# Seven token tiles in place of eight, the last three 512 wide, in a fused attention and two-block feed-forward kernel

## The chip, the cores and the metric

The kernel runs on one core of a Trainium2 chip. The metric is the device time of one execution in microseconds. Three runs of the kernel before took 1172.88, 1173.68 and 1174.52 us (median 1173.68). TensorE is called PE, VectorE DVE, ScalarE ACT, GpSimd POOL and SyncE SP.

## The reference

All inputs are float32. Stage one is a chunked attention over 4 batches, 8 heads, 768 positions of 64 values: the queries of a chunk of 32 positions see 8 memory keys and the keys from 16 positions before the chunk to 8 behind it.

```
scores = q_c @ [mem_k, k_ctx]^T / 8;  a = softmax(scores);  o = a @ [mem_v, v_ctx]
x  = o as 3072 tokens x 512
h  = x @ w_in                          # 512 -> 2048
g  = max(h, 0) + log1p(exp(-|h|))      # softplus
x1 = g @ w_out                         # 2048 -> 512
out = ((x1 @ w_a) * (x1 @ w_b)) @ w_out2   # 512 -> 1536 -> 512
```

## The kernel before, in words

Every product is made of three matmuls on a high and a low part of each operand, which keeps float32 precision.

**Token tiles.** The 3072 tokens are cut into eight tiles of 384 (TT). For each tile t and each of 16 slices f of the hidden dimension one *iteration* runs: `emit_h` (12 matmuls into a PSUM bank `ph`, L563), `emit_soft` (ACT: Abs, Exp, Ln, L570 to L572; DVE: the final step into `g`, L574; ACT: the high part `gh`, L551; POOL, or DVE in the first and last tile: the low part `gl`, L554), and `emit_x1` of the iteration two before (12 matmuls into the four accumulator banks `px`, L587). Behind the last slice of a tile the four accumulators are copied by DVE (L595) and stored to a scratch (L596); that happens in the second iteration of the next tile, and the next tile's first `emit_x1` needs the copied banks.

**Attention beside it.** The attention of later tiles runs inside earlier tiles. It is cut into units of 128 tokens; units 0 to 5 come first, by other code, and units 6 to 23 go through the steps of the class `Unit`: `turn` (DVE transposes of keys and queries, L411 to L414, and two small ACT copies, L416), `scores` (PE, L430), `soft` (8 masked reductions on DVE, L379, and 8 exponentials on ACT, L383), `norm` (DVE, then POOL, L390), `flip` and `flip2` (5 DVE transposes each, L448), `values` (PE, L477, into a bank of the same pair as `ph`), `place` (ACT and DVE, writes the unit into the x tile of a later token tile).

**Order.** Time is counted in slots, two for an iteration: slot 2(16t+f) is reached behind `emit_soft`, the next one behind `emit_x1`. A list `plan` holds (slot, unit, step) and `att_at(slot)` emits what is due. From tile 1 on, SP, PE and DVE run in exactly the order in which the code emits; ACT and POOL are ordered by a planner. `placed[u]` is the slot of a unit's `values`, `scored[u]` that of its `scores` (the slot of `values` of the unit ahead), the others stand at fixed distances (L24, L25, L518). The same list holds `Early`: 30 conversions of later weights, each a fetch, an ACT step (`top`), a DVE step of two instructions (`value`, L685, L686) and a store. Keys and queries are fetched by many small DMAs per group of three units, values by two to four per unit.

**Stage two** takes x1 back in pairs of 512-token tiles and runs 12 slices of a 7-product scheme (L772) and the output product (L795), all with 512 columns.

Of the kernel before, what the change touches and what calls it, by code (L numbers as in the profile page):

```python
# [44 lines left out]
PRE, PRE_BY = 5, 4.2  # L45
PRE_STEPS = (0, 3.4, 4.1, 4.3)
# [4 lines left out]
def attn_moe_moe2(ctx: ExitStack, tc: tile.TileContext, q, k, v, mem_k, mem_v,  # L51
# [14 lines left out]
    UPT = TT // QU  # L66
    BPT = TT // QB
    KS = KB // 32
    NTILE = NT // TT
# [81 lines left out]
    masks = [ap.tile([P, KB], F32, name=f"mask{i}") for i in range(4)]  # L151
# [81 lines left out]
    def x_tile(t):  # L233
        if t not in xt:
            xt[t] = mp.tile([P, 2, KT, TT], F32R, tag="x", name=f"x{t}")
        return xt[t]
# [155 lines left out]
    class Unit:  # L392


        def __init__(self, u):
            self.u = u
            self.b, self.n = divmod(u, NU)
            self.own_bank = False

# [3 lines left out]

        def turn(self):
            u, kn, qn = self.u, loaded.k, loaded.q
# [4 lines left out]
            self.qt = a2.tile([P, KT, QU], F32, tag="qt", name=f"qt{u}", bufs=1)  # L410
# [69 lines left out]
        def place(self):  # L480
            t, c0 = divmod(self.u * QU, TT)
# [20 lines left out]
    placed = {u: 2 * NF1 * (u // UPT - 1) + PLACED[u % UPT] for u in range(2 * UPT, len(units))}  # L502
    scored = {u: placed[u - 1] if u > 2 * UPT else SCORED for u in placed}
    turned = {u: scored[u] + TURN if u > 2 * UPT else TURNED for u in placed}
# [22 lines left out]
    for t in range(2, NTILE):  # L527
# [13 lines left out]
    def turn_of(tag, n, dtype):  # L541

        if tag not in rings:
            rings[tag] = mp.tile([P, n, TT], dtype, tag=tag, name=tag, bufs=1)
# [4 lines left out]
    def split(val, name, engine=nc.gpsimd, between=None):  # L549
        hi, lo = turn_of("gh", 3, F32R), turn_of("gl", 3, F32R)  # L550
        anchor[0] = nc.scalar.copy(hi, val)  # L551
        if between:
            between()
        engine.tensor_tensor(lo, val, hi.bitcast(F32), ALU.subtract)  # L554
        return hi, lo

    def emit_h(t, f):
        x, w = xt[t], w1[f]
        ph = ps.tile([P, 512], F32, tag="h", name=f"ph{t}_{f}")[:, :TT]
# [8 lines left out]
    def emit_soft(t, f, ph, engine=nc.gpsimd, one=None, two=None):  # L568
        e = mp.tile([P, TT], F32, tag="e", name=f"e{t}_{f}")
# [7 lines left out]
        gt[t, f] = split(g, f"g{t}_{f}", engine, two)  # L577

    def emit_x1(t, f):
# [46 lines left out]
    def operand(p, n):  # L626
# [6 lines left out]
        if n in ("11", "s2", "s3"):  # L633
            return [home(f"x{n}", late["x"], [P, KH, 2, T2], f"x{n}")]
        if n == "s1":
            return [home("xs1a", late["x"], [P, 1, 2, T2], "xs1"), home("xa", mp, [P, 3, 2, T2], "x")[:, 0:1]]
        if n == "12":
            return [home("xa", mp, [P, 3, 2, T2], "x")[:, 1:3]]
        if n == "22":
            return [home("xb", mp, [P, 3, 2, T2], "x")[:, 0:2]]  # L640
        return [parts[p, "xb"][:, 2:3], home("xs4b", mp, [P, 1, 2, T2], "gh")]

    def pieces_of(p, n):
        k = 0
        for x in sums[p, n]:
            yield x, raws[n][:, k:k + x.shape[1]]
            k += x.shape[1]

    def split_hi(p, n, copy):
        sums[p, n] = operand(p, n)  # L650
        for x, raw in pieces_of(p, n):
            copy(x[:, :, 0], raw)

    def split_lo(p, n, engine):
        for x, raw in pieces_of(p, n):
            engine.tensor_tensor(x[:, :, 1], raw, x[:, :, 0].bitcast(F32), ALU.subtract)
# [122 lines left out]
    def temp(tag, name):  # L779
        return mp.tile([P, T2], F32, tag=tag, name=name, bufs=2 if tag == "e" else 1)  # L780
# [90 lines left out]
    def order():  # L871
# [62 lines left out]
        n_pre = PRE * (NTILE - 2)  # L934
        for n, e in enumerate(pre[:n_pre]):
            t, i = divmod(n, PRE)
            for d, step in zip(PRE_STEPS, (e.fetch, e.top, e.value, e.store)):
                plan.append((2 * NF1 * (t + 1) + PRE_BY * i + d, 100 + n, step))
# [25 lines left out]
        for t in range(NTILE):  # L964
# [9 lines left out]
            for f in range(NF1):  # L974
                ph = emit_h(t, f)
                if t == 0:
                    fetch_to(ROUNDS_CV + AHEAD + int(len(rest) * (f + 1) / CV_DONE))
                    convert()
                    emit_soft(t, f, ph, nc.vector, convert)
                    convert()  # L980
                elif t < NTILE - 1:
                    emit_soft(t, f, ph)
                else:
                    emit_soft(t, f, ph, nc.vector, partial(slot, 2 * f), partial(slot, 2 * f + 1))
                att_at(2 * (NF1 * t + f))
                if len(pend) >= LAG:
                    emit_x1(*pend.pop(0))
                pend.append((t, f))
                att_at(2 * (NF1 * t + f) + 1)
        def between_0():  # L990
            emit_x1(*pend.pop(0))

        for k in sorted(plan2):
            slot(k)
        for p in range(NPAIR):
            more = p + 1 < NPAIR
            for f in range(NF2):

                def at(k):
# [22 lines left out]
                    if more:  # L1022
# [4 lines left out]
                        if f == NF2 - 1:  # L1027
                            split_hi(p + 1, PRODUCTS[k], nc.scalar.copy)
                            if k > 0:
                                split_lo(p + 1, PRODUCTS[k - 1], nc.gpsimd if k in (2, 4) else nc.vector)  # L1030
                    if f == 0 and k == 0 and p > 0:
                        split_lo(p, PRODUCTS[6], nc.vector)
                    if p == f == 0 and k in (0, 2):
                        split_hi(0, PRODUCTS[5 + k // 2], nc.scalar.copy)
                    if p == f == 0 and k in (1, 3):
                        split_lo(0, PRODUCTS[5 + k // 2], nc.vector)
# [43 lines left out]
```

## Time and profile before

| what | before |
|---|---|
| median of three runs | 1173.68 us |
| the profiled execution | 1173.41 us |
| its span, first to last instruction | 1171.6 us |
| PE busy | 1161.1 us (99%) |
| DVE busy | 724.2 us (62%) |
| ACT busy | 530.7 us (45%) |
| POOL busy | 263.6 us (23%) |
| PE, share of the chain that ended last | 94% |

The profile is of one execution. Between the span and the time lie 1.8 us. A busy PE is a PE with matmuls in flight; the gap from one matmul's start to the next one's is the better measure. The stage of the token tiles lies from 40 to 633 us of the span, stage two behind it.

### The profile page before, as it was taken

The page shows a single profiled execution, that of the slowest core. Times are in us where ns is not written, and L with a number is a line of the kernel's source. Part 1 is how long each engine was busy: PE and PEld are TensorE (multiplying, and loading weights), DVE is VectorE, ACT ScalarE, POOL GpSimd, SP SyncE. Part 2 cuts the span into 40 slices and gives each one's busy share as a digit, 9 for nine tenths or more (in the row PEclk, how much of TensorE's full clock was granted, in tenths as well). Part 3 has the DMA queues.
Part 4 walks back from the last instruction along what each step waited for, and adds up shares of the span by engine and source line. Part 5 has one row for each costly group of instructions (what it writes and reads, how often), then busy time and mean ns, then how long its engine had stood idle before and what let it go on. Part 6 is the DMA issues. An engine that isn't in the chain of part 4 may idle for free.

```text
span 1171.6 us, 20283 instructions
## 1 busy us (share of the span) xinstructions
PE 1161.1 (99%) x7462; PEld 1049.1 (90%) x7462; DVE 724.2 (62%) x1603; ACT 530.7 (45%) x1293; POOL 263.6 (23%) x239
## 2 busy tenths in 40 slices
PE   9899999999999999999999999999999999999998
PEld 7799999999999999999999888888888888888887
DVE  6888655565555655455377567867456657455555
ACT  6899666656666566666565332222211113111110
POOL 2000223233232222322324665710002001000000
PEclk9999999999999999999999999999999999999999
DMA  9955353533534335332474758464854443864301
GB/s 228 301 189 103 90 135 76 132 80 98 132 79 125 81 104 136 75 101 68 140 261 161 274 216 287 171 224 150 339 203 144 152 145 106 305 226 153 135 1 72
DMA packets 193714, 181.47 MB, mean 155 GB/s; under 512 B 123168, under 2 KB 151760, under 8 KB 193616
## 3 DMA queue, kind: packets, MB, share of 16 engines
q1 hardware_dynamic: 193232, 180.13, 49.4%
q8 instruction: 59, 0.97, 0.3%
q14 instruction: 39, 0.32, 0.1%
q0 software_dynamic: 384, 0.05, 0.0%
HBM read 129.79 MB, written 50.33 MB: 154 GB/s over the span
## 4 chain that ended last, share of the span: by engine, by line
PE 94%; DMA 2%; DVE 1%; SPq 1%; ACT 0%; issue 0%; POOL 0%; DVEq 0%; POOLq 0%
PE px L587 22%; PE ph L563 22%; PE py L795 17%; PE pX L772 8%; PE pV L772 8%; PE pW L772 8%; PE pY L772 4%; PE pxa L477 2%; PE sc L430 1%; DMA raw<-in_moe_w_in_dram 1%; DMA vv<-in_v_dram 1%; DMA kp<-in_k_dram 1%; SPq L330 1%; DVE af L448 0%; PE pa L466 0%
## 5 line engine op out<-in xcount | busy, mean ns | idle before, releaser
L563 PE MATMUL ph<-x,w 128*128 128x384 f32 x1536 | 289.4, 336 | 0.1
L587 PE MATMUL px<-gh,w 128*128 128x384 f32 x1024 | 281.5, 335 | 1.4 <-DVE qn L295 1.4
L563 PEld LDWEIGHTS ph<-x,w 128*128 128x128 f32 x1536 | 267.2, 188 | 2.1 <-ACT x L369 0.2
L795 PE MATMUL py<-w2o,c 128*128 128x512 f32 (+1 forms) x870 | 218.0, 388 | 0.0
L795 PEld LDWEIGHTS py<-w2o,c 128*128 128x128 f32 x870 | 162.7, 188 | 33.5
L587 PEld LDWEIGHTS px<-gh,w 128*128 128x128 f32 x1024 | 186.7, 188 | 2.8 <-DVE qn L295 1.8
L574 DVE SCALAR_TENSOR_TENSOR g<-ph,e 128x384 f32<-128x384 f32 x128 | 71.0, 555 | 189.0 <-ACT e L572 184.9
L587 PE MATMUL px<-gl,w 128*128 128x384 f32 x512 | 171.1, 334 | 0.0
L854 ACT CAST c<-r 128x512 fp32r<-128x512 f32 x36 | 22.4, 622 | 308.2 <-DVE r L852 287.2
L554 POOL TENSOR_TENSOR gl<-g,gh 128x384 fp32r<-128x384 f32 x96 | 97.3, 1014 | 222.8 <-ACT gh L551 206.7
L551 ACT CAST gh<-g 128x384 fp32r<-128x384 f32 x128 | 65.6, 513 | 88.4 <-DVE g L574 87.2
L804 DVE TENSOR_TENSOR y<-py,y 128x512 f32<-128x512 f32 (+1 forms) x121 | 82.9, 685 | 36.2 <-PE py L795 36.0
L570 ACT ACTIVATE e<-ph 128x384 f32<-128x384 f32 x128 | 62.3, 486 | 88.4 <-PE ph L563 75.7
L587 PEld LDWEIGHTS px<-gl,w 128*128 128x128 f32 x512 | 96.1, 188 | 0.1
L448 DVE STREAM_TRANSPOSE af<-sm 32x256 f32<-32x256 f32 x180 | 78.2, 434 | 3.6 <-POOL sm L390 1.1
L572 ACT ACTIVATE e<-e 128x384 f32<-128x384 f32 x128 | 67.3, 526 | 3.9
L571 ACT ACTIVATE e<-e 128x384 f32<-128x384 f32 x128 | 67.3, 526 | 3.6
L851 DVE TENSOR_TENSOR d<-pW,q 128x512 f32<-128x512 f32 x36 | 24.9, 691 | 69.1 <-PE pW L772 69.1
L383 ACT ACTIVATE sm<-sm,st 128x96 f32<-128x96 f32 x168 | 60.5, 363 | 5.8 <-DVE st L379 5.8
L772 PE MATMUL pX<-x,u 128*128 128x512 f32 x216 | 54.8, 389 | 0.0
L772 PE MATMUL pW<-xs,u 128*128 128x512 f32 x216 | 54.8, 389 | 0.0
L772 PE MATMUL pY<-xs,u 128*128 128x512 f32 x216 | 54.8, 389 | 0.0
(162 smaller groups left out, 1634.8 us busy)
## 6 DMA issues: line engine op xcount, KB each, us to landing
u<-u_scratch SPq DMA_DIRECT2D x72, 512.0 KB
u_scratch<-u SPq DMA_DIRECT2D x36, 512.0 KB
w2o<-w2o_scratch SPq DMA_DIRECT2D x24, 512.0 KB
raw<-in_moe_w_in_dram SPq DMA_DIRECT2D x16, 512.0 KB
raw<-in_moe_w_out_dram SPq DMA_DIRECT2D x16, 512.0 KB
vn<-in_v_dram SPq DMA_DIRECT2D x35, 176.0 KB
raw_a<-in_moe_w_a_dram SPq DMA_DIRECT2D x12, 512.0 KB
raw_b<-in_moe_w_b_dram SPq DMA_DIRECT2D x12, 512.0 KB
```

The source lines that it names most:

```text
L448: nc.vector.transpose(out=af[32 * kb:32 * kb + 32, x], in_=self.sm[32 * x:32 * x + 32, :, 32 * kb:32 * kb + 32])
L551: anchor[0] = nc.scalar.copy(hi, val)
L554: engine.tensor_tensor(lo, val, hi.bitcast(F32), ALU.subtract)
L563: nc.tensor.matmul(ph, lhsT=w[:, a, kt * P:(kt + 1) * P], rhs=x[:, c, kt, :], start=n == 0, stop=n == 3 * KT - 1)
L570: nc.scalar.activation(e, ph, AF.Abs)
L571: nc.scalar.activation(e, e, AF.Exp, scale=-1.0)
L572: nc.scalar.activation(e, e, AF.Ln, bias=1.0)
L574: nc.vector.scalar_tensor_tensor(g, ph, 0.0, e, ALU.max, ALU.add)
L587: nc.tensor.matmul(acc[t][i][:, :TT], lhsT=a, rhs=c, start=f == 0 and m == 0, stop=f == NF1 - 1 and m == 2)
L772: nc.tensor.matmul(bank[:, :T2], lhsT=u[:, j, a, kt * P:kt * P + P], rhs=x[kt][:, c], start=first_ and m == 0, stop=m == 3 * KH - 1, skip_ ...
L795: nc.tensor.matmul(b, lhsT=c[:, x, r], rhs=w[:, y, cols], start=n == 0, stop=n == 3 * GROUP - 1)
L804: tt(y, b, y, ALU.add)
```

## The change

The token tiles become four of 384 and three of 512 (`WIDTHS`). The slots of `values` are written out by hand (`PLACED`): units 6 to 13 nine slots behind their `scores`, units 14 and 15 ten, units 16 to 23 eight, so that all units are placed by slot 190 of 224 (before: 222 of 256). The queries are turned by a step of their own (`turn_q`), five slots ahead of `scores`. The keys are turned three slots ahead of `scores` (two in 512-wide tiles) in place of two with the queries, and their buffer is now shared with the softmax's `sm`, so that they are turned behind the `flip2` of the unit in front. `flip` and `flip2` stand five and six slots behind `scores` (four and five where the unit has eight). DVE's result `g` is written over `e`; `gh` and `gl` have two buffers in place of three, and are emitted behind the `emit_x1` of the iteration. The copies of the accumulators go to a buffer of `tmp` and one of `e` in turn, behind `gh` and `gl`. The six conversions of a tile stand 5.1 slots apart (before: five, 4.2). In stage two the operands lie in two buffers of four parts, and some splits move by one position at the end of a pair.

```diff
+WIDTHS = (384, 384, 384, 384, 512, 512, 512)
-PLACED = (11, 21, 30)
+PLACED = (43, 52, 61, 70, 79, 88, 97, 106, 116, 126, 134, 142, 150, 158, 166, 174, 182, 190)
 TURNED, SCORED = 32, 34
-TURN, SOFT, NORM, FLIP, FLIP2 = -2, 1, 3, 5, 6
-HALVES = ((0, 8, 0.6), (8, 13, 0.9))
+TURN_Q, TURN, TURN_SOON, SOFT, NORM, FLIP, FLIP2 = -5, -2, -3, 1, 3, 5, 6
+HALVES = ((0, 8, 0.65), (8, 13, 0.9))
-PRE, PRE_BY = 5, 4.2
-PRE_STEPS = (0, 3.4, 4.1, 4.3)
+PRE, PRE_BY = (0, 6, 6, 6, 6, 6, 0), 5.1
+PRE_STEPS = (0, 4.4, 5.0, 5.2)
...
-            sm = a2.tile([P, H, KB], F32, tag="sm", name=f"sm{u}", bufs=1)
-            st = a2.tile([P, 4, H], F32, tag="st", name=f"st{u}")
+            sm = a2.tile([P, H, KB], F32, tag="kt", name=f"sm{u}", bufs=1)
+            st = a2.tile([P, 4, H], F32, tag="st", name=f"st{u}", bufs=1)
...
-    turned = {u: scored[u] + TURN if u > 2 * UPT else TURNED for u in placed}
+    turned = {u: TURNED if u == 2 * UPT else scored[u] + TURN if WIDTHS[units[u - 1].at] == T2 else scored[u] + TURN_SOON
+              for u in placed}
...
-        whens[i] = [(turned[u], "turn"), (at - 0.005, "scores"), (at + SOFT, "soft"), (at + NORM, "norm"),
-                    (max(at + FLIP, to - 7), "flip"), (max(at + FLIP2, to - 5), "flip2"), (to - 0.03, "values"), (to - 0.02, "place")]
+        whens[i] = [(max(at + TURN_Q, TURNED), "turn_q"), (turned[u], "turn"), (at - 0.005, "scores"), (at + SOFT, "soft"), (at + NORM, "norm"),
+                    (at + FLIP - (to - at < 9), "flip"), (at + FLIP2 - (to - at < 9), "flip2"), (to - 0.03, "values"), (to - 0.02, "place")]
...
     def emit_soft(t, f, ph, engine=nc.gpsimd, one=None, two=None):
-        e = mp.tile([P, TT], F32, tag="e", name=f"e{t}_{f}")
+        c = slice(0, WIDTHS[t])
+        e = turn_of("e", 2, F32)[:, c]
+        hi, lo = turn_of("gh", 2, F32R)[:, c], turn_of("gl", 2, F32R)[:, c]
...
-        g = turn_of("g", 2, F32)
-        nc.vector.scalar_tensor_tensor(g, ph, 0.0, e, ALU.max, ALU.add)
+        nc.vector.scalar_tensor_tensor(e, ph, 0.0, e, ALU.max, ALU.add)
...
+        def parts():
+            anchor[0] = nc.scalar.copy(hi, e)
+            if two:
+                two()
+            engine.tensor_tensor(lo, e, hi.bitcast(F32), ALU.subtract)
...
+                elif i % 2 == 0:
+                    o = mp.tile([P, n], F32, tag="tmp", name=f"xo{t}_{i}", bufs=2)
                 else:
-                    o = turn_of("g", 2, F32) if i > 1 else mp.tile([P, TT], F32, tag="e", name=f"xo{t}_{i}")
-                nc.vector.tensor_copy(o, acc[t][i][:, :TT])
-                nc.sync.dma_start(x1d[:, i, TT * t:TT * t + TT], o)
+                    o = turn_of("e", 2, F32)[:, :n]
+                nc.vector.tensor_copy(o, acc[t][i][:, :n])
+                nc.sync.dma_start(x1d[:, i, C0[t]:C0[t + 1]], o)
...
                 att_at(2 * (NF1 * t + f))
-                if len(pend) >= LAG:
-                    emit_x1(*pend.pop(0))
+                done = pend.pop(0) if len(pend) >= LAG else None
+                if done:
+                    emit_x1(*done)
+                parts_()
+                if done:
+                    emit_x1_out(*done)
                 pend.append((t, f))
```

## Rows read from the trace of the kernel before

**Rows 1.** The page: busy time by engine, and the granted clock in 40 slices.
```profile
PE 1161.1 (99%) x7462; PEld 1049.1 (90%) x7462; DVE 724.2 (62%) x1603; ACT 530.7 (45%) x1293; POOL 263.6 (23%) x239
...
PEclk9999999999999999999999999999999999999999
```

**Rows 2.** The page: the chain that ended last, by engine.
```profile
PE 94%; DMA 2%; DVE 1%; SPq 1%; ACT 0%; issue 0%; POOL 0%; DVEq 0%; POOLq 0%
```

**Rows 3.** The chain in order of time: start, us, what; each stage's commonest piece.
```profile
386.23 2.08 PE px L587 x12
...
800.90 1.36 PE py L795 x6
```

**Rows 4.** Waits of PE in the token tiles: total us, times, longest.
```profile
PE px L587 <- DVE qn L295: 1.4, 1, 1.4
...
PE sc L430 <- DVE qt L414: 1.0, 1, 1.0
```

**Rows 5.** Timeline of DVE, 376 to 404 us: start, us, instruction [idle before <- releaser].
```profile
380.40 2.22 DVE L448 STREAM_TRANSPOSE af<-sm 32x256 f32<-32x256 f32 x5
382.65 0.43 DVE L685 TENSOR_SCALAR val_a<-raw_a 128x512 uint32<-128x512 uint32 x1
...
383.91 2.23 DVE L448 STREAM_TRANSPOSE af<-sm 32x256 f32<-32x256 f32 x5
...
386.65 0.70 DVE L411 STREAM_TRANSPOSE kt<-kn 128x512 f32<-128x512 f32 x1
...
387.60 0.67 DVE L414 STREAM_TRANSPOSE qt<-qn 128x512 f32<-128x512 f32 x1
...
390.84 1.04 DVE L686 SCALAR_TENSOR_TENSOR val_b<-raw_b,val_b 128x512 uint32<-128x512 uint32 x1 [0.82 <-ACT raw_b L681]
...
394.75 0.25 DVE L379 CUSTOM_DVE_ANT_0 sm<-sc,mask 128x96 f32<-128x96 f32 x1
...
395.99 0.25 DVE L379 CUSTOM_DVE_ANT_0 sm<-sc,mask 128x96 f32<-128x96 f32 x1
```

**Rows 6.** Timeline of PE at the second tile's end: the group behind h, and two groups later.
```profile
200.52 0.33 PE L587 MATMUL px<-gh,w 128*128 128x384 f32 x1
...
204.68 0.33 PE L587 MATMUL px<-gh,w 128*128 128x384 f32 x1
```

**Rows 7.** Timeline of DVE there: softplus's last step, then the copies.
```profile
202.43 0.56 DVE L574 SCALAR_TENSOR_TENSOR g<-ph,e 128x384 f32<-128x384 f32 x1 [3.25 <-ACT e L572]
202.91 1.01 DVE L595 COPY xo<-px 128x384 f32<-128x384 f32 x2
203.84 0.55 DVE L595 COPY g<-px 128x384 f32<-128x384 f32 x1
```

**Rows 8.** Groups by form: busy us, mean ns of one | idle before.
```profile
L574 DVE SCALAR_TENSOR_TENSOR g<-ph,e 128x384 f32<-128x384 f32 x128 | 71.0, 555 | 189.0 <-ACT e L572 184.9 <-issue 3.4
...
L551 ACT CAST gh<-g 128x384 fp32r<-128x384 f32 x128 | 65.6, 513 | 88.4 <-DVE g L574 87.2
...
L383 ACT ACTIVATE sm<-sm,st 128x96 f32<-128x96 f32 x168 | 60.5, 363 | 5.8 <-DVE st L379 5.8
...
L843 DVE TENSOR_TENSOR r<-pV,r 128x512 f32<-128x512 f32 x36 | 24.9, 692 | 31.6 <-PE pV L772 31.6
...
L854 ACT CAST c<-r 128x512 fp32r<-128x512 f32 x36 | 22.4, 622 | 308.2 <-DVE r L852 287.2 <-issue 21.0
```

**Rows 9.** Timeline of ACT: the next iteration's Abs at that tile's end.
```profile
205.47 0.49 ACT L570 ACTIVATE e<-ph 128x384 f32<-128x384 f32 x1 [1.93 <-DMA x_scratch<-xo]
```

**Rows 10.** Timeline of SP: the copies' stores, and a fetch of queries.
```profile
203.48 0.83 SPq L596 DMA_DIRECT2D x_scratch<-xo  x2
...
401.91 0.43 SPq L191 DMA_DIRECT2D qn<-in_q_dram  x1
```

**Rows 11.** Timeline of ACT: the small key copies of unit 6.
```profile
124.86 0.34 ACT L416 COPY kt<-mem_t 128x32 f32<-128x32 f32 x2 [0.62 <-DVE kt L413]
```

**Rows 12.** Busy time by stretch, inside the first tile: PE, PEld, DVE, ACT, POOL.
```profile
75.00:98.00 23.00, 23.00 (x257) 22.59 (x248) 19.88 (x52) 21.18 (x53) 0.00 (x0) 1.00 0.70 225
```

More of the change, by code (lines that the diff above doesn't have):

```diff
@@ L66, in attn_moe_moe2 @@
     UPT = TT // QU
+    C0 = [sum(WIDTHS[:t]) for t in range(len(WIDTHS) + 1)]
     BPT = TT // QB
     KS = KB // 32
-    NTILE = NT // TT
+    NTILE = len(WIDTHS)
     NPAIR = NT // (2 * T2)
@@ L149, in next_half @@
         return halves[n_half[0] - 1]
-    masks = [ap.tile([P, KB], F32, name=f"mask{i}") for i in range(4)]
+    masks = [ap.tile([P, KB], F32, name=f"mask{i}") for i in range(3)]
+    masks.append(wp.tile([P, KB], F32, tag="w", name="mask3"))
     ident = wp.tile([P, P], F32, tag="w", name="ident")
@@ L480, in place @@
         def place(self):
-            t, c0 = divmod(self.u * QU, TT)
+            t = sum(self.u * QU >= c for c in C0[1:])
+            c0 = self.u * QU - C0[t]
             x = x_tile(t)
@@ L547, in turn_of @@
         return rings[tag][:, n_turn[tag] % n]
[L549 to L555, printed above, removed]
     def emit_h(t, f):
         x, w = xt[t], w1[f]
-        ph = ps.tile([P, 512], F32, tag="h", name=f"ph{t}_{f}")[:, :TT]
+        ph = ps.tile([P, 512], F32, tag="h", name=f"ph{t}_{f}")[:, :WIDTHS[t]]
         n = 0
@@ L624, in add_pair, with operand @@
             engine.tensor_tensor(r["s4"], r["12"], r["s2"], ALU.subtract)
-    def operand(p, n):
+    def operand(p, n, i):
         def home(key, pool, shape, tag):
@@ L633, in operand, with split_hi, split_lo @@
         if n in ("11", "s2", "s3"):
[L634 to L656, printed above, removed]
+            return home(f"x{n}", late["x"], [P, KH, 2, T2], f"x{n}")
+        x = home("xa" if n in ("s1", "12") else "xb", mp, [P, 4, 2, T2], "x")
+        return x[:, 0:2] if n in ("s1", "22") else x[:, 2:4]
+    PIECES = {n: 1 for n in PRODUCTS}
+    def split_hi(p, n, copy, which=(0, 1)):
+        for i in which:
+            if i < PIECES[n]:
+                x = operand(p, n, i)
+                sums.setdefault((p, n), []).append(x)
+                k = x.shape[1]
+                copy(x[:, :, 0], raws[n][:, i * k:i * k + k])
+    def split_lo(p, n, engine, which=(0, 1)):
+        for i in which:
+            if i < PIECES[n]:
+                x = sums[p, n][i]
+                k = x.shape[1]
+                engine.tensor_tensor(x[:, :, 1], raws[n][:, i * k:i * k + k], x[:, :, 0].bitcast(F32), ALU.subtract)
     us, w2o = {}, {}
@@ L779, in temp @@
     def temp(tag, name):
-        return mp.tile([P, T2], F32, tag=tag, name=name, bufs=2 if tag == "e" else 1)
+        if tag == "e":
+            return turn_of("e", 2, F32)
+        if tag == "g":
+            if "r" not in late:
+                late["r"] = late["x"].tile([P, T2], F32, name="r", bufs=1)
+            return late["r"]
+        return mp.tile([P, T2], F32, tag="gl", name=name, bufs=1)
     cs, yacc, jobs, n_jobs = {}, {}, [], [0]
@@ L933, in order @@
         pre = [Early(*divmod(n, 3)) for n in range(3 * NF2)]
-        n_pre = PRE * (NTILE - 2)
-        for n, e in enumerate(pre[:n_pre]):
-            t, i = divmod(n, PRE)
+        n_pre = sum(PRE)
+        for n, (t, i) in enumerate((t, i) for t in range(NTILE) for i in range(PRE[t])):
+            e = pre[n]
             for d, step in zip(PRE_STEPS, (e.fetch, e.top, e.value, e.store)):
-                plan.append((2 * NF1 * (t + 1) + PRE_BY * i + d, 100 + n, step))
+                plan.append((2 * NF1 * t + PRE_BY * i + d, 100 + n, step))
         plan.sort(key=lambda p: p[:2])
@@ L1027, in at @@
                         if f == NF2 - 1:
[L1028 to L1036, printed above, removed]
+                            for n, *which in HIGHS[k]:
+                                split_hi(p + 1, n, nc.scalar.copy, which or (0, 1))
+                            for n, engine in LOWS[k]:
+                                split_lo(p + 1, n, engine)
+                    if f == 0 and p > 0:
+                        for n in HIGHS_0[k]:
+                            split_hi(p, n, nc.scalar.copy)
+                        for n, engine in LOWS_0[k]:
+                            split_lo(p, n, engine)
+                    if p == f == 0:
+                        if k == 0:
+                            split_hi(0, "22", nc.scalar.copy)
+                        if k == 1:
+                            split_lo(0, "22", nc.vector)
+                        if k == 2:
+                            split_hi(0, "s4", nc.scalar.copy)
+                        if k == 3:
+                            split_lo(0, "s4", nc.vector)
                 pair_step(p, f, at, (between_0, between_0) if (p, f) == (0, 0) else ())
```

43 lines of the change are left out of this document (28 added, 15 removed).

## The prediction

> **What bounds the kernel now.** Read the page's busy times first: PE has matmuls in flight for 1161.1 of 1171.6 us, with a granted clock in the top tenth of 2.4 GHz in every slice, and no other engine passes 62% [rows 1]. The chain that ended last says the same: 94% of it is PE [rows 2]. The head up to some 40 us waits for DMA and no edit touches it. Then the chain in order of time: from 40 us on it is one PE group behind another, 2.08 us for 12 matmuls of 384 columns, 1.36 us for 6 of 512 [rows 3]. Last the list of PE's waits: in the token tiles two count, 1.4 us at the first x1 group and 1.0 us at the scores of unit 7, which waited for the queries' transposes [rows 4]. So two things move the time: what PE has to do, and new waits of PE. Idle time of DVE, ACT and POOL is worth nothing by itself.
>
> **Fewer, wider matmuls.** A 384-wide matmul takes 2.08/12 = 173.3 ns, a 512-wide one 1.36/6 = 226.7 ns [rows 3]. The 128 columns between cost 53.3 ns, so 13.3 ns of each matmul do not depend on its width. The tiles of 512 hold 1536 tokens: 4 old tiles x 16 iterations x 24 = 1536 matmuls, now 3 x 16 x 24 = 1152. Removed: 384 x 13.3 ns = **5.12 us**. Check: four old tiles take 4 x 32 x 2.08 = 266.24 us, three new ones 3 x 32 x 2.72 = 261.12. Both widths are measured on the same engine with the same operand types, so I give this term no range.
>
> Both rows contradict a rule of the Trainium skill: "TensorE: Matmul & The Clock Gate", section "Back-to-back issue gap", puts the gap between warm matmuls at columns/2.4 ns plus 2.5 ns. That is 162.5 and 215.8 ns where the trace has 173.3 and 226.7. By it the term would be 384 x 2.5 ns = 0.96 us and the sum below 4.16 us higher; the measurement decides here, and the rule is the last of the rivals.
>
> **The wait at unit 7's scores.** Queries now go first, in time that DVE idles in, and the keys stand a slot earlier. The 1.02 us should go; I take 1.02 (0 to 1.02) [rows 4].
>
> **What the closer attention costs.** PE takes it in order and DVE runs in the written order, so I add up DVE's steps around each place where PE needs one. Prices from start to next start: stt (softplus's last step, L574) 0.48 [rows 7]; flip, flip2 2.25 each, conversion `value` 1.26 (382.65 to 383.91), keys 0.95 (386.65 to 387.60), 8 reductions 1.42 [rows 5]; one x1 copy 0.47, with its end 0.55 [rows 7]. Let T be the moment at which PE leaves h of an iteration. stt starts at T+1.91 (200.52 to 202.43), and the group after next starts at T+4.16 [rows 6, 7]. For 512 columns stt and copies grow by 0.13 (nearest row of 512: 692 ns against 555) and each ACT step by 0.11 (622 against 513), so stt starts at T+2.24 and frees DVE at T+2.85 [rows 8].
>
> 1. *Copies behind a flip.* In the second iteration of a tile the four x1 copies stand behind slot 2 of it, and slots 66, 130 and 162 now hold a flip, slot 98 the reductions. Before, the first copy is out at T+2.94 and PE asks for the bank at T+4.16: 1.2 us to spare. Tile 2: 1.91 + 0.48 + 2.25 + 0.55 = T+5.19, 1.03 late. Tile 3: 1.91 + 0.48 + 1.42 + 0.55 = 4.36, 0.20 late. Tile 4: 2.85 + 2.25 + 0.55 = 5.65 against 2.08 + 2.72 = 4.80, 0.85 late. Tile 5: 5.10 + 0.69 = 5.79 against 5.44, 0.35 late. The later banks follow at PE's pace.
> 2. *Values behind a full iteration.* `values` takes one of the two banks that h uses. At an even slot, h of the same iteration holds the one, so the other must have been read by the stt of the iteration before. Units 7 and 11 (values at slots 52 and 88) have two iterations earlier stt, `value`, flip, flip2 and keys in one iteration: the next stt ends at 1.91 + 0.48 + 1.26 + 2.25 + 2.25 + 0.95 + 0.48 = T+9.58, where PE arrives at 2 x 4.16 = T+8.32. 1.26 late, twice. Unit 9 (slot 70) has the four copies in place of `value`: 10.20 against 8.32 + 1.03, 0.85 late. Unit 13 (slot 106) has neither: 8.32 against 8.32, I take 0.1 (0 to 1.0). Odd slots give PE another 2.08 us and lose nothing.
> 3. *Abs behind a store.* The second copy lies in the buffer that the next Abs writes. Before, Abs waited 1.93 us for such a store, which landed 2.0 us after its issue, and PE did not notice [rows 9, 10]. In tile 5 the copy is out at T+6.4, its store lands near T+8.8, stt ends near T+11.4, and unit 20's values and unit 21's scores, whose keys stand behind that stt, want it near T+11.2: I take 0.5 (0 to 1.2).
> 4. *Scores of unit 6.* Its keys are now turned last, and two ACT copies of 0.34 us follow them before PE can go [rows 11]: 0.25 (0 to 0.5).
>
> Together 2.43 + 3.47 + 0.5 + 0.25 = **6.65 us**.
>
> **Edits at nothing.** The high part must wait for the x1 group of two iterations before, to T+2.08; it waits for stt's end at T+2.39 anyway (2.72 against 2.85 at 512), which is the cover. In the first tile ACT and DVE are busy 21.2 and 19.9 of 23 us [rows 12]; the same steps only change order there: 0 (-0.4 to +1). SP issues a fetch in 0.43 us, and the 32 of a half group fit into the 16 or more slots that they have [rows 10]. Stage two's splits move by one position of 1.36 us with the next product further off: 0 (-0.5 to +1).
>
> **Sum.** -5.12 - 1.02 + 6.65 = +0.51 us. The profiled execution took 1173.41 us, 1.8 us outside its span: 1173.9. It lies 0.27 us under the median of the three runs, 1173.68.
>
> **The rivals.**
> *DVE's pile-ups stay off PE* (faster). For it: with the same order of steps the trace before has one wait of PE on DVE in six tiles, and nine slots are 18.7 us for a unit. Against it: the sums in 1 and 2 use busy times alone, without a single wait of DVE. Without 1 to 4: 1173.41 - 6.14 = 1167.3; if only 2 is absent, 1170.4.
> *The pile-ups are longer* (slower). The `value` step can itself wait for its ACT half: 0.82 us in one row [rows 5]. Where both stand in one slot, DVE stops with the flips behind it. That adds 0.82 each for units 7 and 11 and 0.9 for unit 13; and in tile 3 the last copy needs the low part that frees its buffer, behind a high part that can stand behind 8 exponentials of 363 ns, 2.9 us [rows 8], of which PE feels 1.7. Sum 4.2: 1178.1. It decides as soon as stt of such an iteration ends 0.5 us later than in 2. For it: ACT and POOL are ordered by a planner. Against: ACT has much room in these tiles.
> *Keys land late.* In the 512-wide tiles the last fetches stand behind a conversion's store, one iteration ahead of their transposes; each of two groups could hold DVE, and PE behind it, by 2 us: 1177.9.
> *The fixed part does not go with the count.* If 384 matmuls less give back nothing, 1173.41 - 1.02 + 6.65 = 1179.0; both rows of group 3 stand against it. (By the page's 2.5 ns it is 1178.1.)
>
> **How the numbers follow.** Forecast 0.48, pile-ups off PE 0.22, longer pile-ups 0.25, late keys 0.03, no fixed part 0.02. A measurement of this kernel tells 0.2%, 2.35 us, from no change. Faster by more than that: 0.22, the first rival. Slower: 0.25 + 0.03 + 0.02 and 0.02 from the forecast's upper end, 0.32. Within: 0.46. The range reaches from half way into the first rival to the second one and the bounds of the open terms: 1169.0 to 1178.8; the forecast's own is 1171.6 to 1176.3.
>
> **What would show it.** Right: PE groups of 2.08 and 2.72 us; PE waits on DVE of 1 us at x1 behind tiles 1 and 3, and waits of `values` (pxa) on stt (L574's line) of about 1 us at units 7, 9 and 11; no wait at unit 7's scores. Wrong: PE without waits in tiles 2 to 5 (then near 1167), or waits that repeat with each of the 18 units, or sit on ACT, POOL or a DMA.

## Result: slower, and the profile after

The changed kernel took 1182.35 us (median of four, 1180.40 to 1184.21) beside 1173.54 us of the kernel before: ratio 1.0074, 95% interval 1.0056 to 1.0092. Forecast was no change, 1173.9, and the range ended at 1178.8. The profiled execution took 1184.21 us with a span of 1182.4, so 10.8 us more than the span before.

The page of the kernel after, busy times, granted clock, and the chain by engine:

```profile
PE 1160.9 (98%) x7078; PEld 1001.6 (85%) x7078; DVE 729.5 (62%) x1578; ACT 518.1 (44%) x1224; POOL 257.5 (22%) x221
...
PEclk9999999999899999999999999999999999999999
...
PE 86%; DVE 5%; DMA 3%; ACT 3%; SPq 2%; issue 1%; POOL 0%; DVEq 0%; ACTq 0%
```

PE has 384 matmuls less and is as long busy as before [rows 1], because others took longer at a lower clock (below). In the chain DVE has gone from 1% to 5% [rows 2], and one slice of the clock shows an 8. The groups of matmuls are as long as forecast: the chain in order of time, in a 512-wide tile, has groups of 2.72 us, as worked out from [rows 3]:

```profile
380.17 2.72 PE ph L566 x12
382.88 2.72 PE px L599 x12
```

So the loss is mostly in waits. The list of PE's waits after (total us, times, longest), to be read beside [rows 4]; the scores' wait for the queries' transposes is gone:

```profile
PE pxa L484 <- DVE e L578: 7.6, 5, 2.5
...
PE px L599 <- DVE xo L612: 2.6, 4, 1.3
PE px L599 <- DVE qn L298: 2.2, 2, 1.3
PE ptq L296 <- ACT kn L291: 1.4, 1, 1.4
...
PE sc L437 <- ACT kt L423: 0.5, 1, 0.5
```

PE's timeline, the rows with such a wait: in order the second x1 group of the first tile, unit 7, the copies of tile 2, units 9, 11 and 13, the copies of tile 4, unit 21:

```profile
53.87 0.69 PE L599 MATMUL px<-gh,w 128*128 128x384 f32 x1 [1.27 <-DVE qn L298]
...
170.80 1.15 PE L484 MATMUL pxa<-af,vn 96*64 96x64 f32 x32 [1.80 <-DVE e L578]
...
209.68 0.41 PE L599 MATMUL px<-gh,w 128*128 128x384 f32 x1 [1.27 <-DVE xo L612]
...
214.76 1.15 PE L484 MATMUL pxa<-af,vn 96*64 96x64 f32 x32 [0.68 <-DVE e L578]
...
258.65 1.15 PE L484 MATMUL pxa<-af,vn 96*64 96x64 f32 x32 [2.14 <-DVE e L578]
...
303.36 1.98 PE L484 MATMUL pxa<-af,vn 96*64 96x64 f32 x32 [2.51 <-DVE e L578]
...
369.61 0.47 PE L599 MATMUL px<-gh,w 128*128 128x512 f32 x1 [0.82 <-DVE xo L612]
...
473.09 1.00 PE L437 MATMUL sc<-kt,qt 64*64 64x96 f32 x32 [0.53 <-ACT kt L423]
```

At unit 13 the same 32 matmuls take 1.98 us, at the other units 1.15. The busy times by stretch (PE, PEld, DVE, ACT, POOL, granted clock, DMA share, GB/s) say why:

```profile
42.00:59.00 17.00, 13.40 (x160) 11.67 (x160) 12.72 (x25) 13.44 (x27) 0.00 (x0) 0.90 0.81 266
300.00:312.00 12.00, 9.49 (x92) 8.82 (x92) 6.83 (x27) 5.13 (x18) 1.91 (x2) 0.72 0.42 86
```

Single microseconds in them show 0.50, the lower level:

```profile
54.00:55.00 1.00, 1.00 (x4) 1.00 (x5) 1.00 (x3) 0.77 (x2) 0.00 (x0) 0.50 0.95 344
304.00:305.00 1.00, 1.00 (x24) 1.00 (x22) 0.00 (x0) 1.00 (x3) 0.85 (x1) 0.50 0.26 44
```

PE fell from 2.4 to 1.2 GHz for a while at the waits of 1.27 and 2.51 us. That is 17 x 0.10 = 1.7 us and 12 x 0.28 = 3.4 us of PE's time, a part of it while PE waited anyway; before, both stretches stood at 1.00.

The account of this profile: the first tile's fourth h starts at 58.29 in place of 55.84 (+2.45), stage two from its first product to the end takes 547.4 in place of 546.5 us (+0.9), and the 7.5 us more between them are matmuls -5.12 (as forecast), scores -1.02, copies +2.56 (1.27, 0.16, 0.82, 0.31), `values` +7.57 (units 7, 9, 11, 13 and 0.44 at unit 4), scores of unit 21 +0.53, together 4.5, and a remainder of 3.0, which fits the clock's 3.4 us behind unit 13.

### The profile page after: what moved, and what is told of

The parts are those of the page before. It is cut to its first block, busy times and chain, and to the rows that moved or that the text cites. A ratio compares the mean times of both kernels' runs of the same rounds, so it can differ in the third digit from the quotient of the medians.

```text
span 1182.4 us, 19376 instructions
## 1 busy us (share of the span) xinstructions
PE 1160.9 (98%) x7078; PEld 1001.6 (85%) x7078; DVE 729.5 (62%) x1578; ACT 518.1 (44%) x1224; POOL 257.5 (22%) x221
## 4 chain that ended last, share of the span: by engine, by line
PE 86%; DVE 5%; DMA 3%; ACT 3%; SPq 2%; issue 1%; POOL 0%; DVEq 0%; ACTq 0%
PE px L599 19%; PE ph L566 18%; PE py L815 17%; PE pV L786 8%; PE pW L786 8%; PE pX L786 8%; PE pY L786 4%; PE pxa L484 2%; DVE af L455 2%; PE sc L437 1%; DMA kp<-in_k_dram 1%; SPq L333 1%; DMA raw<-in_moe_w_in_dram 1%; DVE e L578 1%; ACT e L576 1%
## 5 line engine op out<-in xcount | busy, mean ns | idle before, releaser
L566 PE MATMUL ph<-x,w 128*128 128x384 f32 (+1 forms) x1344 | 283.4, 359 | 0.1
L599 PE MATMUL px<-gh,w 128*128 128x384 f32 (+1 forms) x896 | 271.1, 363 | 4.8 <-DVE xo L612 2.6
L566 PEld LDWEIGHTS ph<-x,w 128*128 128x128 f32 x1344 | 241.5, 188 | 23.5 <-issue 0.3
L578 DVE SCALAR_TENSOR_TENSOR e<-ph,e 128x384 f32<-128x384 f32 (+1 forms) x112 | 68.5, 611 | 200.2 <-ACT e L577 199.9
L599 PE MATMUL px<-gl,w 128*128 128x384 f32 (+1 forms) x448 | 161.4, 360 | 0.0
L587 POOL TENSOR_TENSOR gl<-e,gh 128x384 fp32r<-128x384 f32 (+1 forms) x80 | 92.6, 1157 | 248.3 <-ACT gh L584 238.2
L575 ACT ACTIVATE e<-ph 128x384 f32<-128x384 f32 (+1 forms) x112 | 59.7, 533 | 108.8 <-PE ph L566 84.0
L584 ACT CAST gh<-e 128x384 fp32r<-128x384 f32 (+1 forms) x112 | 62.4, 557 | 62.7 <-DVE e L578 42.6
L871 DVE TENSOR_TENSOR d<-pW,e 128x512 f32<-128x512 f32 x36 | 24.9, 691 | 70.5 <-PE pW L786 70.5
L577 ACT ACTIVATE e<-e 128x384 f32<-128x384 f32 (+1 forms) x112 | 63.9, 571 | 3.1
L576 ACT ACTIVATE e<-e 128x384 f32<-128x384 f32 (+1 forms) x112 | 63.8, 570 | 3.3
```

The lines of the kernel that those rows point to most:

```text
L566: nc.tensor.matmul(ph, lhsT=w[:, a, kt * P:(kt + 1) * P], rhs=x[:, c, kt, :], start=n == 0, stop=n == 3 * KT - 1)
L576: nc.scalar.activation(e, e, AF.Exp, scale=-1.0)
L577: nc.scalar.activation(e, e, AF.Ln, bias=1.0)
L578: nc.vector.scalar_tensor_tensor(e, ph, 0.0, e, ALU.max, ALU.add)
L584: anchor[0] = nc.scalar.copy(hi, e)
L587: engine.tensor_tensor(lo, e, hi.bitcast(F32), ALU.subtract)
```

## Experiments

Each was timed in five rounds beside the kernel before; "gain" is e0_again's median less the run's. The kernel before had medians of 1172.5 to 1173.5 in these rounds, so a gain is good to about 1 us.

**e0_again**: the changed kernel, unaltered.

> The changed kernel unaltered, timed anew. Theory (three parts): PE's new waits on DVE cost about 12.9 us in its first profile, 1.0 us of old waits and 5.1 us of matmuls are gone, and in two places the granted clock falls after a wait (0.90 in 42 to 59 us, 0.72 in 300 to 312 us, where the kernel before has 1.00), which costs the other 4 us. If all three hang on the written order, this profile shows the same places and sizes to 0.3 us and 1180 to 1184 us. Rival: the fall of the clock and the head's extra 2.5 us are chance of the one profiled execution; then the clock is 1.00 in both windows here, and the time nearer 1178.

Measured: 1181.15 us, ratio 1.0069 (1.0053 to 1.0084). The waits stand at the same places with the same sizes to 0.1 us (units 7, 9, 11, 13: 1.81, 0.68, 2.15, 2.43). The clock is another matter: it fell again in the first tile, but then behind unit 11 (1.7 us) and not behind unit 13. So the waits repeat with the written order, and what the clock adds to them changes from run to run. Of the ten executions of this kernel on record, two had a granted clock of 1.000 over the whole span and took 1180.40 and 1177.75 us; the other eight, at 0.996 to 0.998, took 1179.94 to 1184.21.

**e1_head**: the old order in the first two iterations.

```diff
-                    parts_ = emit_soft(t, f, ph, nc.vector, convert, convert)
+                    parts_ = emit_soft(t, f, ph, nc.vector, convert, convert if f >= LAG else None)
+                    if f < LAG:
+                        parts_()
+                        convert()
+                        parts_ = list
```

> The changed kernel, with the first two iterations of the first tile in the order of the kernel before (high and low part and both conversion steps ahead of the slot with the packed turns). Theory: the new order lets the third turn's queries copy and its ACT copy come late, PE waits 1.41, 0.92 and 1.27 us and then runs 3 us at the lower clock; with the old order h(3) starts again near 56 us in place of 58.3, the granted clock in 42 to 59 us is 1.00, and the time is 2 to 2.5 us below the changed kernel's: about 1180. Rival: the packed rows land 1.2 us later by DMA, whatever the order; then h(3) starts at 57 us or later and the time falls by 1.2 us at most.

Measured: 1181.90 us, 1.0076 (1.0063 to 1.0089): no gain, so the theory falls. ACT's timeline, the weight for which it waits in the first tile, in the kernel after and in e1_head:

```profile
42.68 0.67 ACT L119 ACTIVATE raw<-raw 128x512 f32<-128x512 f32 x1 [3.90 <-DMA raw<-in_moe_w_in_dram]
```
```profile
42.65 0.68 ACT L119 ACTIVATE raw<-raw 128x512 f32<-128x512 f32 x1 [3.56 <-DMA raw<-in_moe_w_in_dram]
```

Over all 16 profiles of this study that step starts between 39.62 and 42.68 us (before: 41.45), and the fourth h starts 14.2 to 14.4 us behind it where the clock is 1.00 from 50 to 62 us, 15.5 to 15.7 where it is 0.86 (the kernel after, e0_again, e3b_order, e3c_anchor). So no cost of the order in the head is seen: the start follows one landing, which varies by 3 us, and the clock.

**e2_no_value**: the 30 DVE steps `value` left out (the words stored are those of another weight).

```diff
     def value(self):
+        if "x" not in late:
+            self.val = w1[0][:, 0].bitcast(U32)
+            return
```

> The changed kernel without the two DVE steps (1.26 us together) of each of the 30 conversions that run beside the token tiles; the stored words are those of another weight, so that the transfer stays. Theory: these steps are the part of DVE's pile-ups that makes `values` late at units 7, 11 and 13 (waits of PE 1.80, 2.14 and 2.51 us): they become 0.5, 0.9 and under 1.2 us, unit 9 (0.68) stays, as do the x1 copies (1.27 and 0.82), and with the wait at unit 13 the stretch of 0.72 granted clock behind it goes (2.9 us): 1182.4 - 1.3 - 1.3 - 1.4 - 2.9 = 1175.5. Rival 1 (the wait of Abs for the store of an x1 copy makes unit 13 late, not `value`): unit 13 keeps 1.5 us or more and the clock still falls, 1179. Rival 2 (DVE's load does not set these waits, ACT or the fetches do): no wait changes by over 0.3 us, 1182.

Measured: 1173.51 us, 1.0009 (1.0000 to 1.0018), a gain of 7.6. PE's timeline at units 7, 11 and 13:

```profile
165.85 1.15 PE L484 MATMUL pxa<-af,vn 96*64 96x64 f32 x32 [0.74 <-DVE e L578]
...
252.52 1.15 PE L484 MATMUL pxa<-af,vn 96*64 96x64 f32 x32 [0.94 <-DVE e L578]
...
295.37 1.15 PE L484 MATMUL pxa<-af,vn 96*64 96x64 f32 x32 [0.69 <-DVE e L578]
```

Against e0_again 1.07, 1.21 and 1.74 us are gone, and the clock is 1.00 from 42 to 480 us. PE's waits behind 60 us fell from 10.4 to 6.7 us, which is 3.7 of the 7.6. The rest does not come from these waits: the clock differs, and so does the head, which the steps left out do not touch (the fourth h at 54.40 in place of 57.62). At unit 13, where the prediction had no `value` in the sum, it is worth the most. DVE's timeline there, in the kernel after:

```profile
292.74 0.56 DVE L578 SCALAR_TENSOR_TENSOR e<-ph,e 128x384 f32<-128x384 f32 x1 [3.40 <-ACT e L577]
...
294.16 1.35 DVE L699 TENSOR_SCALAR val_a<-raw_a 128x512 uint32<-128x512 uint32 x1
295.62 1.32 DVE L700 SCALAR_TENSOR_TENSOR val_a<-raw_a,val_a 128x512 uint32<-128x512 uint32 x1
...
297.32 4.47 DVE L455 STREAM_TRANSPOSE af<-sm 32x256 f32<-32x256 f32 x10
```

and POOL's, of the same time:

```profile
293.76 1.47 POOL L393 TENSOR_TENSOR sm<-sm,st 128x768 f32<-128x768 f32 x1 [5.93 <-DVE st L391]
295.19 1.20 POOL L587 TENSOR_TENSOR gl<-e,gh 128x384 fp32r<-128x384 f32 x1
```

`value` took 2.67 us in place of 1.1: its first half ended 0.28 us behind the end of POOL's `norm`, its second 0.55 us behind the low part's. The whole trace repeats this: of the steps `value` from 130 to 640 us, 4 first halves and 7 second halves began 0.07 us or more behind the start of a POOL step that was still at work. They ended 0.28 to 0.29 and 0.54 to 0.56 us behind that step's end and took 0.71 to 1.49 and 1.02 to 1.67 us. All others took 0.39 to 0.43 and 0.69 to 0.70, also where a POOL step began with them or later. The Trainium skill says in "SBUF — State Buffer", section "SBUF: two separate sides", that VectorE and GpSimd share a pair of ports: a GpSimd step that reads SBUF and a VectorE step with two inputs in SBUF, or one in a mode that uses both ports, exclude each other, and the later one stands still. The trace agrees for the second half, which has two inputs in SBUF; the first half has one, and no run shows its mode.

The pile at unit 13 begins further ahead. ACT's timeline, the Abs for the stt at 292.74:

```profile
291.11 0.49 ACT L575 ACTIVATE e<-ph 128x384 f32<-128x384 f32 x1 [1.55 <-DMA x_scratch<-e]
```

ACT had the eight exponentials until 289.56, then Abs waited for the store of tile 3's second x1 copy. PE had left h at 287.94, so by T+1.91 stt was due at 289.85; it came 2.9 us late, and `norm` and `value` behind it. A late stt alone cost little: in e2 it was 2.3 us late, and unit 13 waited 0.69 us; in e8c_spread_anchor, with `value` ahead of it, it was 2.3 us late, and unit 13 did not wait. A held `value` behind a punctual stt at this place was not run; by the sum, 289.85 + 0.48 + 0.94 + 2.70 = 293.97, it would be done before the next stt is due at 294.27.

**e6_copies_first**: the flip ahead of the x1 copies in tiles 2, 4 and 5 moved behind them.

```diff
-(at + FLIP - (to - at < 9), "flip")
+(at + FLIP - (to - at < 9) + 0.5 * (at in (61, 126, 158)), "flip")
```

> The changed kernel, with the flip that stands ahead of the four x1 copies in tiles 2, 4 and 5 moved behind them, half a slot. Theory A: what PE waits for is DVE's sum over an iteration or two, not one step; the copies' waits (1.27, 0.82 and 0.31 us) go, but the flip and the next stt come as much later, and `values` of unit 9 waits 1.9 to 2.1 us in place of 0.68, that of unit 16 0.8 to 1.2 in place of none: no gain, within 0.5 us of the changed kernel's 1181.2. Theory B: each wait stands by itself, as the sum in the prediction had it: 2.4 us less, 1178.8.

Measured: 1180.37 us, 1.0078 (1.0056 to 1.0100), nearer to theory A (1181.2) than to B (1178.8), and the waits decide for A. The copies' waits went and came up at `values` of unit 9 (0.68 before) and of unit 16 (none before):

```profile
213.69 1.15 PE L484 MATMUL pxa<-af,vn 96*64 96x64 f32 x32 [2.54 <-DVE e L578]
...
371.87 1.15 PE L484 MATMUL pxa<-af,vn 96*64 96x64 f32 x32 [1.27 <-DVE e L578]
```

**e8_spread**: all the work, the conversions at other times.

```diff
+PRE_AT = (31.5, 37.1, 42.2, 47.3, ...
...
-PRE_STEPS = (0, 4.4, 5.0, 5.2)
+PRE_STEPS = (0, 3.4, 4.1, 4.3)
...
```

> The changed kernel with all its work, but the 30 conversions set at other times (4.6 to 7.6 slots apart in place of 5.1), so that none of their DVE steps falls into the two iterations ahead of `values` of units 7, 11 and 13. Theory: only where the step stands counts, not that it is there: waits at units 7, 11 and 13 of 0.1, 0.4 and 0.5 us or less (worked out by adding up DVE's and ACT's steps in order) in place of 1.8, 2.15 and 2.4, unit 9 and the copies as in the changed kernel, the granted clock 1.00 from 60 to 480 us: 1181.2 - 5.4 - 1.7 = 1174, as without the steps (1173.5). Rival 1: the load as such is too much, the waits come up at other units: 1178 or more. Rival 2: the raw words land late at the closer spacings (as in e3_order, 0.5 to 3.4 us), and `value` holds DVE for them: waits at other units that begin with ACT's wait for a DMA, 1177 to 1183.

Measured: 1182.42 us, 1.0085 (1.0069 to 1.0101): no gain; rival 2, and more. ACT waited nine times for raw words, and unit 7's wait rose to 3.22 us because a `value` now ran beside `norm`, 1.67 + 1.38 us.

**The order by itself: e3_order, e3b_order, e3c_anchor, e3d_order, e3d_anchor.** Eight tiles of 384 with the schedule of the kernel before, but the order and the buffers of the change.

```diff
-WIDTHS = (384, 384, 384, 384, 512, 512, 512)
+WIDTHS = (384,) * 8
-PLACED = (43, 52, 61, ...
+PLACED = tuple(32 * t + n for t in range(1, 7) for n in (11, 21, 30))
...
```

> The changed kernel's order of steps and its buffers (high part behind the x1 group, x1 copies behind it in two homes, queries apart from keys, keys a slot earlier), but with eight tiles of 384 and the unit places, flips and conversion times of the kernel before. Theory: the cost sits in the tighter places of the units, not in the order; here only the head's 2.5 us and the scores' gain of 1.0 us are left: 1175.0 (1174 to 1176.5), no wait of PE over 0.5 us behind 60 us. Rival: the order itself (high part later, Abs behind a store, two buffers where three were) makes PE wait in each tile: 1178 or more, with waits of x1 or values in most tiles.

Measured: 1188.35 us, 1.0129 (1.0107 to 1.0151): the theory falls for this kernel. The queries had come into the flips' iteration, and ACT waited up to 3.4 us for raw words. e3b_order was to take both away (queries, fetches and masks as before):

> e3_order was 15.9 us slower than the kernel before, with 12 waits of `values`; but there the queries had come into the flips' iteration, and the words of a weight landed up to 3.4 us after ACT was ready for them, which neither belongs to the order of the softplus's parts. Here, with eight tiles of 384 and the units, conversions, queries, keys, fetches and masks of the kernel before, only that order and its buffers are left: high part and low part behind the x1 group, x1 copies behind both, two homes of each kind. Theory: this order costs nothing: 1172 to 1174.5 beside 1172.5 of the kernel before, no wait of `values` over 0.5 us, no wait of ACT for raw words. Rival: the order costs by itself (Abs behind the store of an x1 copy, two homes in place of three): 1176 or more, with waits at x1 or `values` in most of six tiles.

Measured: 1190.47 us, 1.0151 (1.0135 to 1.0166). Two causes were still mixed. The queries stood a slot later than in the kernel before, behind one stt more; and ACT, of which this is the timeline, went on waiting:

```profile
216.46 0.49 ACT L574 ACTIVATE e<-ph 128x384 f32<-128x384 f32 x1 [0.66 <-PE ph L565]
216.99 0.53 ACT L575 ACTIVATE e<-e 128x384 f32<-128x384 f32 x1
218.65 0.66 ACT L694 ACTIVATE raw_a<-raw_a 128x512 f32<-128x512 f32 x1 [1.14 <-DMA raw_a<-in_moe_w_a_dram]
219.22 0.51 ACT L576 ACTIVATE e<-e 128x384 f32<-128x384 f32 x1
```

The conversion's ACT step `top` (L694) stands here between Exp and Ln of the iteration in which it is written. In the code it is tied (`issue_after(anchor[0].ins)`) to the high part written last. Before, that is the high part of the same iteration, behind its stt. Since the change writes the high part behind the slot, it is that of the iteration before, and the planner may take `top` up to an iteration earlier, ahead of the steps that stt needs. e3c_anchor, e3d_anchor, e8c, e9 and e10 tie it to Ln of its own iteration:

```diff
-        nc.scalar.activation(e, e, AF.Ln, bias=1.0)
+        anchor[0] = nc.scalar.activation(e, e, AF.Ln, bias=1.0)
...
-            anchor[0] = nc.scalar.copy(hi, e)
+            nc.scalar.copy(hi, e)
```

> e3b_order with one thing more: the ACT step of a conversion (`top`) is tied to Ln of the iteration that it is written in, and not to the high part. In the order of the change the high part written last is that of the iteration before, so ACT took `top` up to an iteration earlier, ahead of Exp and Ln, and stood there for the raw words (0.5 to 1.8 us, 9 times in e3b_order). Theory: that is all that the order costs; no wait of ACT for raw words, no waits of the scores for the queries (14.1 us in e3b_order): 1173 to 1175. Rival: the order costs in another way too (stores of x1 copies, two homes, keys and softmax in one home); waits of 4 us or more remain: 1178 to 1188.

Measured: 1182.32 us, 1.0069 (1.0053 to 1.0086): 8 us less, but the scores still waited 7.9 us for the queries. With the queries back in place, without and with the new tie:

> e3b_order with the queries where the kernel before has them, in the slot of the keys and ahead of them (in e3b_order they stood a slot later, behind one stt more, which by itself gave the scores waits of 0.98 us at up to 8 units). Theory: what is left is the cost of `top` tied to the high part of the iteration before: late stt, some 1 us each at part of the 18 units: 1178 to 1184. Rival: the queries' place was the whole cost: 1173 to 1175.

Measured: 1175.43 us, 1.0020 (1.0009 to 1.0031), between theory and rival.

> e3d_order with `top` tied to Ln of its own iteration. Theory: with this and with the queries in place, the order of the change and its two homes cost nothing: no wait of the scores over 0.5 us, 1172 to 1175. Rival: Abs behind the store of an x1 copy, and keys and softmax in one home, cost by themselves: 1177 or more.

Measured: 1171.81 us, 0.9995 (0.9985 to 1.0006). So the order and its two homes show no cost once the two things beside it are right; the tie to the high part costs 3.6 us here (1175.43 against 1171.81), and queries one slot late cost 10.5 with the new tie in place (1182.32 against 1171.81).

**e10_after_anchor**: the changed kernel with the new tie only.

> The changed kernel with `top` tied to Ln of its own iteration and nothing else. Theory: the changed kernel writes `top` a slot later (4.4 in place of 3.4), which covers the tie; its profile has one wait of ACT for raw words (0.7 us) and its waits are sums of DVE steps: no gain, 1180 to 1182. Rival: the tie is the cause of the waits at units 7, 11 and 13 here too: 1175 or less.

Measured: 1178.18 us, 1.0045 (1.0032 to 1.0059), a gain of 3.0: between the two. Unit 7 now waits 1.25 us in place of 1.80, unit 11 1.65 in place of 2.14. But unit 13 waits 2.64 us, and a wait for the low part is new (PE's list, two of its lines):

```profile
PE pxa L484 <- DVE e L578: 6.7, 5, 2.6
...
PE px L599 <- POOL gl L587: 0.5, 1, 0.5
```

All waits behind 60 us come to 10.2 us beside 10.4 in e0_again. So the tie moves two waits, and the gain of 3.0 is not shown to be its own: in this profile the clock stood at 1.00 from 42 to 480 us, and the weight's landing in the first tile came at 40.01 in place of 41.91 us. ACT's timeline ahead of unit 7, the kernel after, then e10_after_anchor:

```profile
160.77 0.49 ACT L575 ACTIVATE e<-ph 128x384 f32<-128x384 f32 x1 [1.14 <-PE ph L566]
161.16 0.51 ACT L584 CAST gh<-e 128x384 fp32r<-128x384 f32 x1
161.56 0.67 ACT L695 ACTIVATE raw_o<-raw_o 128x512 f32<-128x512 f32 x1
162.13 0.51 ACT L576 ACTIVATE e<-e 128x384 f32<-128x384 f32 x1
```
```profile
156.86 0.49 ACT L575 ACTIVATE e<-ph 128x384 f32<-128x384 f32 x1 [0.58 <-PE ph L566]
157.24 0.51 ACT L584 CAST gh<-e 128x384 fp32r<-128x384 f32 x1
157.65 0.53 ACT L576 ACTIVATE e<-e 128x384 f32<-128x384 f32 x1
```

`top` holds Exp for 162.13 - 161.56 = 0.57 us, and that much later stt starts and PE goes on. Without it the wait is 1.25 us where the prediction had 1.26, partly by luck: stt starts at T+2.16 in place of T+1.91 (the high part still stands ahead of Exp), and the steps behind it are 0.15 us shorter than summed. At unit 11 a transpose of the memory keys (0.31 us) stands in the pile as well; from stt's start to the next one's end it is 7.85 us there and 7.51 at unit 7, as the waits differ (2.14 and 1.80).

**e8c_spread_anchor**: e8_spread with the new tie.

> e8_spread (the changed kernel with its conversions at other times) with `top` tied to Ln of its own iteration. In e8_spread ACT waited for raw words 9 times (0.6 to 2.5 us) ahead of Exp and Ln, and units 7 and 11 lost as much as they had won. Theory: those waits go; what is left is that of unit 9 (0.7), the copies (2.6), units 7, 11 and 13 with 0.1, 0.3 and 0.5 us: 1174 to 1176. Rival: the conversions cost wherever they stand, 1179 or more.

Measured: 1176.09 us, 1.0023 (1.0014 to 1.0032), a gain of 5.1. Unit 13 is free of its wait, unit 11 has 0.93; unit 7 keeps 1.87, with `value` beside `norm` (1.67 + 1.32 us, against 0.42 + 0.69 where it stands free). ACT still waited nine times for raw words (0.3 to 3.5 us): the tie does not take these waits away, it puts them behind Ln, and PE's waits behind 60 us fell from 12.0 to 7.4.

**e4_eased** and **e9_eased_anchor**: units, flips and conversions set by adding up DVE's and ACT's steps; e9 with the new tie.

```diff
-PLACED = (43, 52, 61, 70, 79, 88, 97, 106, 116, 126, 134, ...
+PLACED = (44, 53, 62, 72, 80, 89, 99, 108, 116, 125, 134, ...
...
+SHIFT = {6: (1.5, 1.0), 7: (0, -0.5), 8: (-0.5, 0), ...      # flip, flip2 of a unit
...
+PRE_AT = (34.0, 38.6, 44.2, 50.3, 55.4, ...
...
```

> The changed kernel with all its work, but units, flips and conversions set so that no two iterations in a row hold more DVE work than PE's time: places of the units moved by up to 2 slots, flips by up to 1.5, conversions as needed. Theory: all waits of PE in tiles 1 to 5 come from such sums and go, to 0.7 us in all (9.5 to 10 in the changed kernel), and the granted clock stays at 1.00 from 60 to 480 us; what the wider matmuls and the scores of unit 7 give back (5.1 + 1.0) is then seen: 1172.5 - 6.1 + 0.7 + 0.3 = 1167.4 (1166 to 1170). Rival: ACT (Abs behind the stores of x1 copies), the two-deep homes or late raw words set a floor of their own: waits of 3 us or more remain, 1171 or more. Second rival: the fixed part of a matmul does not come back: no waits, and still 1172.

Measured: 1174.76 us, 1.0013 (1.0004 to 1.0022), a gain of 6.4 of the 13.7 expected; 5.8 us of waits were left, half of them behind ACT's waits for raw words.

> e4_eased with `top` tied to Ln of its own iteration. e4_eased had 5.8 us of waits left (units 10, 13 and 14 with 1.36, 0.83 and 0.49 behind ACT's waits for raw words; scores behind ACT's copies of the memory keys 1.6). Theory: the raw words' part goes, 2.5 to 3 us: 1171 to 1172.5, and waits of 2 to 3 us are left. Rival: these waits have another cause, the time stays at 1174.8.

Measured: 1169.31 us, 0.9967 (0.9954 to 0.9979): faster than both kernels. PE's waits behind 60 us, and the clock:

```profile
PE pxa L487 <- DVE e L582: 1.8, 4, 0.9
...
PE sc L440 <- ACT kt L426: 0.2, 1, 0.2
```
```profile
PEclk9999999999999999999999999999999999999999
```

It also bears out the matmuls, beside e3d_anchor, which has 384 more of them. PE's timeline, the first tile's fourth h and stage two's first product, in e9_eased_anchor, then in e3d_anchor:

```profile
55.38 2.35 PE L570 MATMUL ph<-x,w 128*128 128x384 f32 x12
...
620.92 1.52 PE L790 MATMUL pX<-x,u 128*128 128x512 f32 x6
```
```profile
53.89 2.35 PE L565 MATMUL ph<-x,w 128*128 128x384 f32 x12
...
623.03 1.55 PE L785 MATMUL pX<-x,u 128*128 128x512 f32 x6
```

Between the two lie 565.5 and 569.1 us, 3.6 less, with 2.0 us of waits in place of 1.0. So the matmuls gave back some 4.6 us of the 5.12. The medians differ by 2.5 us only, as they also hold the first tile, whose start varies, and stage two (547.5 in place of 546.6).

## Why the prediction failed

**The step that failed** is 2, "values behind a full iteration": 3.47 us were forecast, 7.13 came. "Unit 13 (slot 106) has neither: I take 0.1 (0 to 1.0)" became 2.51, "1.26 late, twice" became 1.80 and 2.14. That DVE's steps over two iterations make `values` late at units 7, 9 and 11 was right, and so was unit 9 (0.85, came 0.68); the prices were not, and at unit 13 the window was too short:
- `value` was priced at 1.26 from one place [rows 5]. Begun behind a POOL step it was 2.67 to 3.05. A longer price stood in the rows: the second half at 390.84 took 1.04 us, and the prediction read only the wait ahead of it. At unit 13 `value` stood beside `norm`, an iteration ahead of the two that had been added up (e2: 1.74 us of the wait; e8c).
- It reached past the time at which the next stt was due because the stt ahead of it was 2.9 us late, behind an Abs that waited for the store of an x1 copy. Step 3 had this mechanism, but summed it for tile 5 only.
- stt was set at T+1.91 from an iteration in which ACT had the softplus alone [rows 6, 7]. The moved high part pulls `top` into the chain, 0.57 us (e10). The prediction followed the high part's own cover ("it waits for stt's end anyway") and not what is tied to it.
- A transpose of the memory keys (0.31 us) stands in the pile of unit 11 and was left out.

**What stood in no step: the clock.** The sum took PE's waits as they are. At waits of 1.3 to 3.2 us the granted clock fell in some places of some runs; some 1.2 and 3.0 us of it reached the time of the profiled run. The Trainium skill says in "TensorE: Matmul & The Clock Gate", section "What's actually happening", that an idle PE falls to 1.2 GHz; the trace agrees that it falls, and shows it at a wait of 1.27 us.

**The first tile at "0 (-0.4 to +1)"** came out 2.45 late in the profile, but not by the order (e1): 1.2 by a landing (42.68 for 41.45) and 1.2 by the clock. These, stage two's 0.9 (taken at 0) and unit 4's 0.44 (in no step) make up with the above the 10.8 us of the profiled execution, where 0.51 were forecast.

**Right:** the matmuls (-5.12; some 4.6 by e9), unit 7's scores (-1.02), the copies (2.43, came 2.56: 1.27, 0.16, 0.82, 0.31 for 1.03, 0.20, 0.85, 0.35), fetches at nothing, stage two inside its bounds (0.9). Unit 6's scores (0.25) did not wait. The rule of the Trainium skill that the prediction set beside the matmuls ("TensorE: Matmul & The Clock Gate", section "Back-to-back issue gap") is given there for a matmul by itself, so the rows do not contradict it; by it 0.96 us would have come back.

Unit 21's scores (0.5, came 0.53) came in part by the step named: Abs waited 5.02 us for the store, DVE stood idle for 0.76 us ahead of that stt, and the keys behind it ended at 472.07. The copy of the memory keys on ACT, for which PE waited, began only at 472.83, behind the high part, `top` and the next Abs. Each of the two 0.76 us is longer than PE's wait.

e6 shows what the sum of single waits hid: they come from one sum of DVE over two iterations, so moving one step moves the wait. The second rival, "longer pile-ups", was the near one. Its place at unit 13 was right and its reason there (a `value` that waits for its ACT half) was not; it did look for trouble behind the eight exponentials of tile 3, though at the last copy and not at Abs.

## What to carry over

Where two engines run in written order, add up their steps over every window of two iterations, with the longest measured price of each step (beside its neighbours on POOL and ACT), and look a step further back than the window: a step that is late there, behind a store, moves all that follows into the window. When a step moves, look for what is tied to it or planned by it, not only for what it waits for. A wait of PE can cost more than its length, since the clock may fall behind it.

## What was not expected of the hardware

Whether the clock falls behind a wait differs from run to run of the same kernel: in e0_again 2.15 us at unit 11 were followed by 1.2 GHz and 2.43 us at unit 13 were not; in e6_copies_first three waits of 2.1 to 2.6 us (units 9, 11 and 13) left it at 1.00; the 1.27 us in the first tile were followed by a fall in four of ten profiles. What decides is left open. The two DVE steps of `value` took 2 to 3 times as long when they began behind a POOL step (1.35 and 1.32 us for 0.43 and 0.69) and not when they began ahead of one; the flips were not held (4.47 us for ten, with POOL's low part from 298.10 to 299.12 inside).
